# A tuned attention-and-MLP kernel in another hand-written order: which engine scales w_in, which engine forms q's long product, and the order of the loads

## The chip, the cores and the metric

The kernel runs on one core of a Trainium2 chip. The metric is the device time of one execution in microseconds, of which the median of three runs stands below. A core has five engines that work side by side, each through its own queue in order: TensorE (PE, matrix products), VectorE (DVE), ScalarE (ACT), GpSimd (POOL) and SyncE (SP, which here only issues loads and stores). An instruction that waits holds up all that stands behind it in its engine's queue.

## The reference, cut to what matters

```python
def phi(x):                                   # S1, S2: (8, 32)
    a = np.einsum('rd,bhsd->bhsr', S1, x)
    b = np.einsum('rd,bhsd->bhsr', S2, x)
    return np.einsum('bhsi,bhsj->bhsij', a, b).reshape(*x.shape[:-1], 64)
q_p, k_p = phi(q), phi(k)                     # q, k, v: (4, 4, 1088, 32)
kv  = np.einsum('bhsf,bhsd->bhfd', k_p, v)
num = np.einsum('bhsf,bhfd->bhsd', q_p, kv)
den = np.einsum('bhsf,bhf->bhs', q_p, k_p.sum(2))[..., None] + 1e-06
x   = (num / den) as 4352 tokens x 128
h   = x @ w_in                                # 128 x 2048
out = (h / (1 + exp(-beta * h))) @ w_out      # 2048 x 128
```

## The kernel before, in words

There are two parts. The **attention part** works on one batch b (0 to 3) at a time: k is loaded and transposed on VectorE (`kT`, L457), projected on TensorE (`kps`, L475), brought back on VectorE (`kab`, L489), multiplied out to 64 features on GpSimd or VectorE (`kp`, L512, in pieces of 256, 512 or 768 elements a partition), and summed against v on TensorE (`kvz`, L536). q goes the same way (`qT` L463, `qps` L596, `qab` L608, `qo` L512, `qt` L639) and ends in a product on TensorE (`nps`, L652) that is copied into the token-major input of the MLP (`xT`, L664). Batch 0 takes a shorter way for its first 512 tokens: features on TensorE (L684), a product `nps` L814, and VectorE writes `xT` (L825). In between stand the denominators: `dpr` (L616, a product of two tiles in SBUF), its sum `rc` (L626) and reciprocal (L629), and the scaling of `qab` (L634).

The **MLP part** takes nine chunks of tokens, eight of 512 and one of 256. For each chunk it goes over w_out's and w_in's 16 blocks of 128 in pairs: W (`first`, L433) is two matmuls into one of two PSUM buffers called wave, G (`silu`, L449) is ScalarE's Silu on 1024 elements a partition, V (`second`, L400) is two matmuls that add into `moeout`. There are 68 of each, and the stores of a chunk follow as E0 to E8 (L414 and L379).

Since the Silu has a factor beta, w_in is multiplied by beta ahead (`winp`, L342: eight parts of 256 columns, u + engine letter + part: `up3` is part 3 by GpSimd, `uv4` part 4 by VectorE) and w_out is divided by it (`woutp`, L351 on ScalarE as wa0 to wa15, L358 on GpSimd as wp). The first two W of a chunk read the parts 0 and 1 of `winp`, the next two 2 and 3, and so on.

What stands in which engine's queue, and in which order, is written out by hand: `SEQ` is a list of short names, the kernel calls one function for each (the table `DO`), and each call appends its instructions to its engine's queue. A name such as `v06` is batch 0's kv piece 6, `op10` the k product of batch 1, piece 0, on GpSimd, `ov10` the same on VectorE, `yp00` the q product of batch 0, piece 0, `t00` its transpose, `np0` two turns for `nps`, `nA` and `xA` the product L814 and the `xT` L825, `n0` to `n3` the products L652, `h` one matmul on a constant (L196) that only keeps TensorE busy. Loads are names too: `li0` to `li2` load w_in's columns 0 to 511, 512 to 1023 and 1024 to 2047, `lo` w_out, `lk`, `lq`, `lv` a batch of k, q, v. SyncE issues them in that order, and the program lets each load wait until the one eight places ahead of it has landed. The products `kp` have one buffer: the first of a batch waits until the `kvz` matmuls of the batch before have read the last.

Of the kernel before, what the change touches and what calls it, by code (L numbers as in the profile page):

```python
# [18 lines left out]
SEQ = """
    lqA lq0 h li0 h li1 h lk1 sp lv0 bsv h h s0 h sw h s1 tk0b be0 sk h tk0a h bc0 h li2 h h bc1 tqA  # L20
    h sr lo1 kp0 tq0 src up0 h lk2 ka0a bA up1 ka0b aA ca0a lo0 ov04 gr0 op02 cA0 ov03 ov00 h op01 h
    be1 ztv op06 gdv0 lq1 tk1 bc2 h op05 h lv1 h ca0b zm cA1 op08 h mA0 bc3 h op07 v03 v05 mA1 wm0
    kp1 zc up3 wc0 v01 rb dA ka1 up2 v02 h h iA lo2 up7 v07 v08 v00 wa6 wa7 v04 up5 qp0 lq2 wa4 wa5
    v06 gr1 qa00 kd0 op13 kda0 qa01 nd0 h gdv1 h tk2 nc0 h lv3 h nA wa2 wa3 dpp0 wm1 h op10 wc1 h xA
    wa0 wa1 np0 h di0 nca0 W op12 W tq1 G kp2 asp0 h G W ov11 h v12 uv4 lo3 G W yv00 v13 G lv2 W ka2
    yp01 h v10 t00 G v11 qp1 up6 t01 kda1 W op22 wa10 wa11 qa11 h G V qa10 op23 lk3 W np1 lq3 tq2 n0
    G dpp1 ncv1 W ov21 xa01 V xa00 op20 di1 G W V G asp1 z20 W V wp4 G W yp13 V G W z21 v23 G W yp12
    v22 G W yp10 v21 t13 zm2 G W wz2 V yp11 G t10 W v20 t12 wa12 wa13 wp7 qp2 t11 G V qa20 V kda2
    qa21 n1 E0 dpv2 V di2 xa10 V W xv11 asp2 V G tk3 W yp22 V G W tq3 kp3 G W yv21 V G W yp20 ka3 V
    G W yp23 t20 V G V W E1 np2 op32 W G t21 V ncv2 V G ov31 W V op33 t22 G W t23 V G W op30 V G W  # L30
    v33 z30 G W V G n2 z31 v31 xa21 W V G W xv20 zm3 v30 G W wz3 V G qp3 E2 v32 qa31 W V qa30 G W V
    dpv3 G W di3 V G kdv3 W asp3 V G yp31 W V G W yp32 V G W yv33 V G V yp30 W E3 np3 W G t31 V ncv3
    V G t32 W V t30 G W t33 V G W V G V W V G W V G n3 E4 W xa31 V G xv30 W V G V W V G W V G W V G
    W V G W V G W E5 V G W V G W V G V W V G W V G W V G W V G W E6 V G W V G W V G W V G W V G W V
    G W V G V W E7 V G V V V E8
"""


# [919 lines left out]
```

## Time and profile before

| | us |
|---|---|
| median of 3 runs (103.78 to 104.2) | 103.98 |
| the profiled execution | 103.7 |
| its span in the trace | 101.9 |
| busy in it: TensorE / ScalarE / VectorE / GpSimd | 96.3 / 79.1 / 64.0 / 41.0 |
| first W starts | 19.55 |
| last V ends | 98.1 |

The span is the trace from the first instruction to the last; 1.8 us of the execution's time lie around it. Before the first W lies the start (loads, beta, batch 0's k and first 512 tokens of q); behind it W, G and V alternate, and the attention of the other batches is laid between them.

### The profile page before, as it was taken

To read this page: it belongs to the slowest core of one execution; us is meant where nothing else is said; L and a number is where in the kernel's file an instruction comes from. 1 tells how busy PE (TensorE), PEld (TensorE's weight loads), DVE (VectorE), ACT (ScalarE), POOL (GpSimd) and SP (SyncE) were. 2 spreads that over 40 slices of the span, in tenths; PEclk is the share of its full clock that TensorE was granted. 3 is DMA by queue.
4 is the path that set the end of the run, shared out by engine and by line. 5 is a ranking of instruction groups with operands and counts; after the bars stand their busy time and mean duration, and the time that the engine had idled before them with its cause. 6 is when DMAs were issued, how large, how long until landed. Compare 5 with 4: busy or idle time off the path is not lost.

```text
span 101.9 us, 2974 instructions
## 1 busy us (share of the span) xinstructions
PE 96.3 (95%) x1225; PEld 48.4 (47%) x1225; DVE 64.0 (63%) x105; ACT 79.1 (78%) x110; POOL 41.0 (40%) x60
## 2 busy tenths in 40 slices
PE   5999999998999999999999999999999999999940
PEld 2465556435353454434544544454454444446730
DVE  2389989999999999995999578358032020020210
ACT  1553618699589995599997859999969999999920
POOL 7306998993976980499800001960000000000000
PEclk9999999999999999999999999999999999999996
DMA  1999999954738100330320000506012306014054
GB/s 29 306 264 385 415 398 378 358 176 149 214 71 330 68 6 0 60 52 0 57 46 6 0 9 10 90 0 103 0 19 31 60 6 100 0 24 71 8 88 67
DMA packets 23576, 11.35 MB, mean 111 GB/s; under 512 B 19323, under 2 KB 21387, under 8 KB 23563
## 3 DMA queue, kind: packets, MB, share of 16 engines
q1 hardware_dynamic: 22419, 11.08, 39.2%
q10 hardware_dynamic: 1144, 0.09, 0.8%
q8 instruction: 9, 0.15, 0.6%
q14 instruction: 4, 0.03, 0.1%
HBM read 8.94 MB, written 2.23 MB: 110 GB/s over the span
## 4 chain that ended last, share of the span: by engine, by line
PE 88%; DVE 7%; issue 0%
PE wave L433 30%; PE moeout L400 29%; PE kvz L196 8%; PE nps L652 6%; PE kvz L536 4%; PE qps L596 3%; PE kps L475 2%; DVE qo L512 1%; DVE winp L342 1%; DVE qT L463 1%; PE aps L684 1%; PE ndps L577 1%; DVE kp L512 1%; DVE kab L489 1%; PE gram L714 1%; PE kvz L714 1%
## 5 line engine op out<-in xcount | busy, mean ns | idle before, releaser
L449 ACT ACTIVATE g<-wave 128x1024 f16<-128x1024 f32 x68 | 64.8, 1036 | 4.8 <-PE wave L433 4.7
L433 PE MATMUL wave<-xT,winp 128*128 128x512 f16 (+1 forms) x144 | 40.6, 369 | 0.0
L400 PE MATMUL moeout<-g,woutp 128*128 128x512 f16 (+1 forms) x144 | 38.4, 367 | 0.1
L433 PEld LDWEIGHTS <-winp 128*128 128x128 f16 x144 | 15.2, 115 | 15.4 <-issue 5.3
L414 DVE STREAM_TRANSPOSE o_sb<-moeout 128x512 f32<-128x512 f32 (+1 forms) x9 | 6.1, 683 | 26.1 <-PE moeout L400 26.1
L400 PEld LDWEIGHTS <-woutp 128*128 128x128 f16 x144 | 13.8, 97 | 14.8 <-issue 0.8
L512 POOL TENSOR_TENSOR kp<-kab 128x256 f32<-128x256 f32 (+2 forms) x15 | 14.3, 976 | 1.9 <-DVE kab L489 1.6
L512 POOL TENSOR_TENSOR qo<-qab 128x512 f32<-128x512 f32 (+1 forms) x11 | 13.9, 1295 | 0.2
L196 PE MATMUL kvz<-idle 128*128 128x400 f16 x40 | 10.8, 381 | 1.2 <-DVE idle L115 1.1
L639 DVE STREAM_TRANSPOSE qt<-qo 128x512 f32<-128x512 f32 (+1 forms) x14 | 10.1, 753 | 0.0
L634 POOL TENSOR_TENSOR qab<-qab,rc 128x288 f32<-128x288 f32 (+1 forms) x4 | 2.5, 632 | 18.7 <-DVE rc L629 18.7
L523 DVE TENSOR_REDUCE zs<-kp 128x128 f32<-128x1152 f32 x4 | 8.4, 2145 | 0.0
L536 PEld LDWEIGHTS kvz<-kp,v 128*32 128x32 f32 x288 | 4.9, 109 | 5.7 <-issue 3.9
L536 PE MATMUL kvz<-kp,v 128*32 128x64 f32 x288 | 7.3, 224 | 0.0
L342 POOL TENSOR_TENSOR winp<-w_in_sb,beta_bc 128x256 f16<-128x256 f32 x7 | 5.1, 753 | 5.2 <-DMA w_in_sb<-in_moe_w_in_dram 5.2
L196 PEld LDWEIGHTS <-idle 128*128 128x128 f16 x40 | 3.8, 109 | 4.7 <-issue 2.5
L652 PE MATMUL nps<-qt,nd 32*32 32x288 f32 (+1 forms) x256 | 6.0, 386 | 0.0
L664 ACT CAST xT<-nps 128x576 f16<-128x576 f32 (+1 forms) x5 | 2.8, 553 | 3.7 <-PE nps L652 3.6
L463 DVE STREAM_TRANSPOSE qT<-q 128x1088 f32<-128x1088 f32 (+2 forms) x5 | 5.2, 1047 | 0.4 <-DMA q<-in_q_dram 0.4
L457 DVE STREAM_TRANSPOSE kT<-k 128x1088 f32<-128x1088 f32 (+2 forms) x5 | 5.4, 1074 | 0.0
L608 DVE STREAM_TRANSPOSE qab<-qps 128x576 f32<-128x576 f32 (+1 forms) x8 | 5.2, 683 | 0.3 <-PE qps L596 0.2
L351 ACT ACTIVATE woutp<-w_out_sb,rbeta 128x128 f16<-128x128 f32 x12 | 4.1, 396 | 1.6 <-DMA w_out_sb<-in_moe_w_out_dram 1.6
(102 smaller groups left out, 71.1 us busy)
## 6 DMA issues: line engine op xcount, KB each, us to landing
v<-in_v_dram SPq DMA_DIRECT2D x15, 144.0 KB, 5.7
k<-in_k_dram SPq DMA_DIRECT2D x3, 544.0 KB, 6.5
q<-in_q_dram SPq DMA_DIRECT2D x3, 544.0 KB, 7.5
out_dram<-o_sb SPq DMA_DIRECT2D x20, 64.0 KB, 2.0
w_out_sb<-in_moe_w_out_dram SPq DMA_DIRECT2D x4, 256.0 KB, 6.6
w_in_sb<-in_moe_w_in_dram SPq DMA_DIRECT2D x2, 256.0 KB
w_in_sb<-in_moe_w_in_dram SPq DMA_DIRECT2D x1, 512.0 KB
k<-in_k_dram SPq DMA_DIRECT2D x1, 288.0 KB, 2.8
```

The source lines that it names most:

```text
L196: nc.tensor.matmul(out=kvz0[:, HC : HC + 400], lhsT=idle, rhs=cut(idle, [[0, 25], [1, 16]]), start=fresh, stop=True, skip_group_check=True,)
L342: eng.tensor_tensor(out=winp[:, c0:c1], in0=w_in_sb[:, c0:c1], in1=beta_bc[:, c0:c1], op=MUL)
L400: nc.tensor.matmul(out=moe["acc"][:, :tw], lhsT=woutp[:, j, :], rhs=g[jj], start=(j == 0), stop=(j == NJ - 1),)
L414: nc.vector.transpose(out=o_sb[:, :nt, :].rearrange("p t d -> p (t d)"), in_=PS["acc", ci][:, :tw])
L433: nc.tensor.matmul(out=wv[:, jj // per, o : o + tw], lhsT=cut(winp, [[step, P]], c), rhs=xT[:, t0 : t0 + tw], start=True, stop=True,)
L449: nc.scalar.activation(out=g, in_=wv, func=ACTF.Silu)
L463: nc.vector.transpose(out=qT2[b % 2][:, t0:t1].rearrange("p t s -> p (t s)"), in_=q_t[b][:, t0:t1].rearrange("p t d -> p (t d)"),)
L512: eng.tensor_tensor(out=cut(dst[b][:, j0:j1], [[F, n], [R, R], [1, R]]), in0=left, in1=cut(a0, [[w, n], [0, R], [1, R]], o + R), op=MUL,)
L523: nc.vector.tensor_reduce(out=RB["zs", b][:, hs].rearrange("p h f -> p (h f)"), in_=KP[b][:, :, hs].rearrange("p j h f -> p (h f) j"), axi ...
L536: nc.tensor.matmul(out=KVZ[b][32 * h : 32 * h + 32, :F], lhsT=v_t[b][:, h, j, :], rhs=KP[b][:, j, h, :], start=(b > 0 and summed[b] == 0), ...
L639: nc.vector.transpose(out=QT[b][:, j0:j1].rearrange("p j h c s -> p (j h c s)"), in_=QO[b][:, j0:j1].rearrange("p j h f -> p (j h f)"),)
L652: nc.tensor.matmul(out=ts[g // 2][32 * h : 32 * h + 32, g % 2, : 32 * nq], lhsT=ND[b][rows, fc, 32 * h : 32 * h + 32], rhs=QT[b][rows, :nq ...
```

## The change

Only `SEQ` is changed. All functions stay, and the set of steps is nearly the same: of w_in's parts, 2, 3, 6 and 7 are now VectorE's (before: only 4), and 4 is GpSimd's; batch 0's nine k products are all GpSimd's (three were VectorE's); its long q product is GpSimd's (`yp00`); batch 0's `dpr` and scaling are VectorE's (`dpv0`, `asv0`); batch 1's `xT` is copied by ScalarE alone; three more `h`. The rest is another order. The two lists, the part up to the product `n0` of batch 0:

```diff
-    lqA lq0 h li0 h li1 h lk1 sp lv0 bsv h h s0 h sw h s1 tk0b be0 sk h tk0a h bc0 h li2 h h bc1 tqA
...
-    v06 gr1 qa00 kd0 op13 kda0 qa01 nd0 h gdv1 h tk2 nc0 h lv3 h nA wa2 wa3 dpp0 wm1 h op10 wc1 h xA
-    wa0 wa1 np0 h di0 nca0 W op12 W tq1 G kp2 asp0 h G W ov11 h v12 uv4 lo3 G W yv00 v13 G lv2 W ka2
-    yp01 h v10 t00 G v11 qp1 up6 t01 kda1 W op22 wa10 wa11 qa11 h G V qa10 op23 lk3 W np1 lq3 tq2 n0
+    lqA lq0 h li0 h lk1 h lk2 h h lv0 bsv h h tk0a be0 h tk0b sp bc0 h li2 h sk h bc1 tqA h h s1 lo0
...
+    op05 sr tk1 h src op04 h bc3 h h h bc2 lo1 op06 zm mA0 lv1 h op02 h tk2 h wm0 kp1 op07 zc wc0
+    v06 dA op03 ka1 v07 h op00 v08 iA v04 v01 v05 v03 v00 lo2 qp0 v02 gr1 lo3 qa00 kd0 qa01 nd0 h
+    lq3 gdv1 h dpv0 nc0 wa0 wa1 uv2 nA uv3 wm1 h wc1 xA h h h lq2 h di0 h h wa4 wa5 W uv7 lk3 W ca0b
+    asv0 wa2 wa3 lv2 up5 h kda0 ov10 ca0a G np0 h op13 G W h kp2 wa6 wa7 up4 W G ka2 op12 tq1 nca0 G
+    op11 v10 v12 yp00 v11 qp1 v13 W kda1 uv6 V t00 yp01 G op20 qa11 qa10 W V ov22 G V t01 wp4 W wa14
+    wa15 tq2 op23 n0 G wa10 wa11 V dpp1 xa01 np1 W op21 xa00 di1 nca1 V G V asp1 z20 W wp6 G yp12 V
```

First VectorE's queue around `xT` of the first 512 tokens (`gd` is a mask on batch 1's gram, `rc` batch 0's denominators). Before:

```order
L608 STREAM_TRANSPOSE qab<-qps 128x2x5x32 x2
L734 TENSOR_TENSOR gd_429<-gram,mh 128x32
L457 STREAM_TRANSPOSE kT_112<-k 128x1088
L825 TENSOR_TENSOR xT<-nps,rb 128x512
L626 TENSOR_REDUCE rc<-dpr_114 128x20
L629 RECIPROCAL rc<-rc 128x20
```

Of the change, the same place:

```order
L608 STREAM_TRANSPOSE qab<-qps 128x2x5x32 x2
L734 TENSOR_TENSOR gd_418<-gram,mh 128x32
L616 TENSOR_TENSOR dpr_114<-qab 128x20x8
L342 TENSOR_TENSOR winp<-w_in_sb,beta_bc 128x256 x2
L825 TENSOR_TENSOR xT<-nps,rb 128x512
L626 TENSOR_REDUCE rc<-dpr_114 128x20
L629 RECIPROCAL rc<-rc 128x20
L342 TENSOR_TENSOR winp<-w_in_sb,beta_bc 128x256
L634 TENSOR_TENSOR qab<-qab,rc 128x20x8
L512 TENSOR_TENSOR kp<-kab 128x512
L489 STREAM_TRANSPOSE kab<-kps 128x2x9x32
L463 STREAM_TRANSPOSE qT_115<-q 128x1088
```

Ahead of `xT`, batch 2's transpose of k went (it now stands earlier), and a `dpr` and two parts of `winp` (2 and 3) came; behind it come another part, the scaling and a k product.

Then GpSimd's queue from its first parts of `winp` on. Before:

```order
L342 TENSOR_TENSOR winp<-w_in_sb,beta_bc 128x256 x2
L512 TENSOR_TENSOR kp<-kab 128x256 x6
L342 TENSOR_TENSOR winp<-w_in_sb,beta_bc 128x256 x4
L512 TENSOR_TENSOR kp<-kab 128x768
L146 MEMSET v 32x64
L616 TENSOR_TENSOR dpr_114<-qab 128x20x8
L512 TENSOR_TENSOR kp<-kab 128x512 x2
L634 TENSOR_TENSOR qab<-qab,rc 128x20x8
```

Of the change:

```order
L342 TENSOR_TENSOR winp<-w_in_sb,beta_bc 128x256 x2
L512 TENSOR_TENSOR kp<-kab 128x256 x9
L342 TENSOR_TENSOR winp<-w_in_sb,beta_bc 128x256
L512 TENSOR_TENSOR kp<-kab 128x768
L342 TENSOR_TENSOR winp<-w_in_sb,beta_bc 128x256
L512 TENSOR_TENSOR kp<-kab 128x512 x2
L512 TENSOR_TENSOR qo<-qab 128x768
L512 TENSOR_TENSOR qo<-qab 128x512
```

Batch 0's products are nine instead of six, and around batch 1's 768-wide product stand two parts of `winp` and the two 512-wide products, in one row.

Last SyncE's loads, from w_in's first one (`li0`) on. Before:

```order
L167 DMA w_in_sb<-in_moe_w_in_dram 128x512 x2
L122 DMA k<-in_k_dram 128x1088
L151 DMA v<-in_v_dram 128x1x288 x4
L167 DMA w_in_sb<-in_moe_w_in_dram 128x1024
L172 DMA w_out_sb<-in_moe_w_out_dram 128x512
L122 DMA k<-in_k_dram 128x1088
```

Of the change:

```order
L167 DMA w_in_sb<-in_moe_w_in_dram 128x512
L122 DMA k<-in_k_dram 128x1088 x2
L151 DMA v<-in_v_dram 128x1x288 x4
L167 DMA w_in_sb<-in_moe_w_in_dram 128x1024
L172 DMA w_out_sb<-in_moe_w_out_dram 128x512
L167 DMA w_in_sb<-in_moe_w_in_dram 128x512
```

Batch 2's k moved up into the place of w_in's second load, which now goes out behind w_out's first and eight places behind batch 1's k.

More of the change, by code (lines that the diff above doesn't have):

```diff
@@ L19 @@
 SEQ = """
-    lqA lq0 h li0 h li1 h lk1 sp lv0 bsv h h s0 h sw h s1 tk0b be0 sk h tk0a h bc0 h li2 h h bc1 tqA
-    h sr lo1 kp0 tq0 src up0 h lk2 ka0a bA up1 ka0b aA ca0a lo0 ov04 gr0 op02 cA0 ov03 ov00 h op01 h
-    be1 ztv op06 gdv0 lq1 tk1 bc2 h op05 h lv1 h ca0b zm cA1 op08 h mA0 bc3 h op07 v03 v05 mA1 wm0
-    kp1 zc up3 wc0 v01 rb dA ka1 up2 v02 h h iA lo2 up7 v07 v08 v00 wa6 wa7 v04 up5 qp0 lq2 wa4 wa5
-    v06 gr1 qa00 kd0 op13 kda0 qa01 nd0 h gdv1 h tk2 nc0 h lv3 h nA wa2 wa3 dpp0 wm1 h op10 wc1 h xA
@@ L25 @@
-    wa0 wa1 np0 h di0 nca0 W op12 W tq1 G kp2 asp0 h G W ov11 h v12 uv4 lo3 G W yv00 v13 G lv2 W ka2
-    yp01 h v10 t00 G v11 qp1 up6 t01 kda1 W op22 wa10 wa11 qa11 h G V qa10 op23 lk3 W np1 lq3 tq2 n0
-    G dpp1 ncv1 W ov21 xa01 V xa00 op20 di1 G W V G asp1 z20 W V wp4 G W yp13 V G W z21 v23 G W yp12
-    v22 G W yp10 v21 t13 zm2 G W wz2 V yp11 G t10 W v20 t12 wa12 wa13 wp7 qp2 t11 G V qa20 V kda2
-    qa21 n1 E0 dpv2 V di2 xa10 V W xv11 asp2 V G tk3 W yp22 V G W tq3 kp3 G W yv21 V G W yp20 ka3 V
@@ L30 @@
[L30 to L34, printed above, removed]
@@ L35 @@
-    G W V G V W E7 V G V V V E8
+    lqA lq0 h li0 h lk1 h lk2 h h lv0 bsv h h tk0a be0 h tk0b sp bc0 h li2 h sk h bc1 tqA h h s1 lo0
+    s0 kp0 tq0 sw up1 aA li1 ka0b bA up0 ka0a h rb cA1 h op01 gr0 cA0 mA1 op08 h lq1 be1 gdv0 ztv
+    op05 sr tk1 h src op04 h bc3 h h h bc2 lo1 op06 zm mA0 lv1 h op02 h tk2 h wm0 kp1 op07 zc wc0
+    v06 dA op03 ka1 v07 h op00 v08 iA v04 v01 v05 v03 v00 lo2 qp0 v02 gr1 lo3 qa00 kd0 qa01 nd0 h
+    lq3 gdv1 h dpv0 nc0 wa0 wa1 uv2 nA uv3 wm1 h wc1 xA h h h lq2 h di0 h h wa4 wa5 W uv7 lk3 W ca0b
@@ new lines @@
+    asv0 wa2 wa3 lv2 up5 h kda0 ov10 ca0a G np0 h op13 G W h kp2 wa6 wa7 up4 W G ka2 op12 tq1 nca0 G
+    op11 v10 v12 yp00 v11 qp1 v13 W kda1 uv6 V t00 yp01 G op20 qa11 qa10 W V ov22 G V t01 wp4 W wa14
+    wa15 tq2 op23 n0 G wa10 wa11 V dpp1 xa01 np1 W op21 xa00 di1 nca1 V G V asp1 z20 W wp6 G yp12 V
+    W z21 V yp10 G W v23 G W yp13 E0 G zm2 v20 v21 t10 W yp11 wz2 V G t12 W V t11 G lv3 qp2 t13 v22
+    W qa21 V G qa20 V W tk3 dpp2 n1 G di2 V xa10 tq3 V asp2 xa11 W yp20 V kdv2 G W np2 yp22 G W V G
@@ new lines @@
+    yp23 W E1 kp3 G W ka3 V G t22 W op33 V ncv2 G V t23 W op30 t20 W G V op31 G W V G op32 V W yp21
+    W z30 G V G W V G t21 W v33 E2 G W z31 V G n2 zm3 xa21 W V xv20 G W wz3 V G W V G qp3 v32 qa31 W
+    V qa30 G W V dpv3 G W di3 V G W asv3 V G W E3 v31 v30 G yv32 W kdv3 yp31 V G W V yv33 G W V t32
+    G W t33 V G W yv30 V G np3 t30 W V t31 G W ncv3 V G V W E4 n3 G W xa31 V G xv30 W V G V W V G W
+    V G W V G W V G W V G W E5 V G W V G W V G W V G W V G W V G W V G W V G W E6 V G V W V G W V G
@@ L36 @@
+    W V G W V G W V G V W E7 V G V V V E8
 """
```

## The prediction, made before the changed kernel ran

> **What bounds the kernel now.** I began with the page: the share of each engine, the slices, the chain that ended last.
>
> ```profile
> PE 96.3 (95%) x1225; PEld 48.4 (47%) x1225; DVE 64.0 (63%) x105; ACT 79.1 (78%) x110; POOL 41.0 (40%) x60
> PE   5999999998999999999999999999999999999940
> DVE  2389989999999999995999578358032020020210
> ACT  1553618699589995599997859999969999999920
> POOL 7306998993976980499800001960000000000000
> PE 88%; DVE 7%; issue 0%
> ```
>
> TensorE is busy from end to end and is 88% of the chain; VectorE's 7% must lie somewhere, and the chain in order of time says where. Its columns are start, duration and what ran; I took one row from each turn.
>
> ```profile
> 18.75 0.69 DVE xT L825
> 23.12 1.41 DVE qo L512
> 26.61 0.18 PE kvz L196
> 28.20 1.10 PE nps L652 x58
> 65.04 0.48 PE wave L433 x2
> 65.52 0.43 PE moeout L400 x2
> 74.03 1.53 PE nps L652 x63
> 98.13 0.45 DVE o_sb L414
> ```
>
> The chain passes through VectorE at `xT`, which lets the first W go, and in the stretch behind it. From 28.20 on it is TensorE alone. So I cut the span at three marks (first W, end of batch 0's product, end of batch 3's) and asked for the busy time of each stretch: length, then TensorE, its weight loads, VectorE, ScalarE, GpSimd.
>
> ```profile
> 19.55:29.31 9.76, 9.22 (x208) 4.39 (x207) 9.73 (x13) 8.21 (x12) 7.85 (x9) 1.00 0.55 172
> 29.31:75.56 46.25, 46.23 (x593) 21.66 (x594) 36.16 (x50) 39.99 (x46) 19.81 (x19) 1.00 0.23 49
> 75.56:98.13 22.57, 22.53 (x117) 11.89 (x116) 2.91 (x5) 21.20 (x23) 0.00 (x0) 1.00 0.25 39
> ```
>
> Behind 29.31 TensorE has no gap worth the name, and the granted clock (third from last) is 1.00. The matmuls behind the first W are the same in both programs. So the kernel's end is the start of the first W, plus a nearly fixed 78.58 us, and the change is decided by what happens to `xT` near 18.75. What can be won behind it is 0.54 us of gaps in the first stretch, and what W pairs of 0.48 lose against 0.43 (0.05 each, a dozen between 61 and 74: 0.6).
>
> **The change part by part: the start.** Now the instructions just ahead of the first W, from the timeline, on all engines.
>
> ```profile
> 16.09 0.32 PE L536 MATMUL kvz<-kp,v 128*32 128x64 f32 x8
> 16.34 0.77 PE L714 MATMUL gram<-kab 128*64 128x32 f32 x18
> 16.58 1.51 POOL L512 TENSOR_TENSOR kp<-kab 128x768 f32<-128x768 f32 x1 [0.28 <-POOL winp L342]
> 17.15 0.19 DVE L734 TENSOR_TENSOR gd<-gram,mh 128x32 f32<-128x32 f32 x1
> 17.98 0.66 PE L814 MATMUL nps<-qp,nd 64*32 64x256 f32 x16
> 18.75 0.69 DVE L825 TENSOR_TENSOR xT<-nps,rb 128x512 f16<-128x512 f32 x1 [0.19 <-PE nps L814]
> 19.55 1.03 PE L433 MATMUL wave<-xT,winp 128*128 128x512 f16 x4
> 20.18 4.92 ACT L449 ACTIVATE g<-wave 128x1024 f16<-128x1024 f32 x5 [0.23 <-PE wave L433]
> 10.01 3.54 POOL L512 TENSOR_TENSOR kp<-kab 128x256 f32<-128x256 f32 x6
> ```
>
> Before, batch 0's kvz ends at 16.41, GpSimd's 768-wide product starts 0.17 later because it takes the buffer that those matmuls read, gram ends near 17.11, VectorE's `gd` follows at 17.15, and `xT` waits for `nps` only.
>
> In the change GpSimd makes nine products in place of six: 10.01 + 9 x 3.54 / 6 = 15.32, and the last kvz must follow them. TensorE's own list (the same matmuls, be1 and qps at other places) comes there at 16.2 to 16.5. I take 16.5: no term. The three more `h` (0.18 each at 26.61 above) lie in the same list ahead of the first W, two of them in its wait for `xT`; without that wait they would cost 0.2 to 0.5. The `nps` then ends near 18.5, 0.2 earlier than before.
>
> What is new is VectorE's queue: `dpr` and two `winp`, all with both inputs in SBUF, stand ahead of `xT`, while GpSimd runs products. The trace of before has that meeting once, at 21 to 24.5.
>
> ```profile
> 20.90 0.47 POOL L634 TENSOR_TENSOR qab<-qab,rc 128x160 f32<-128x160 f32 x1
> 21.09 0.82 DVE L512 TENSOR_TENSOR kp<-kab 128x512 f32<-128x512 f32 x1
> 21.44 1.39 POOL L512 TENSOR_TENSOR qo<-qab 128x512 f32<-128x512 f32 x1
> 21.84 1.28 DVE L342 TENSOR_TENSOR winp<-w_in_sb,beta_bc 128x256 f16<-128x256 f32 x1
> 22.80 0.92 POOL L342 TENSOR_TENSOR winp<-w_in_sb,beta_bc 128x256 f16<-128x256 f32 x1
> 23.04 1.49 DVE L512 TENSOR_TENSOR qo<-qab 128x768 f32<-128x768 f32 x1
> ```
>
> Read the ends: GpSimd's 21.37, VectorE's 21.91, GpSimd's 22.83, VectorE's 23.12, GpSimd's 23.72, VectorE's 24.53. The two never work together; each starts, stands until the other's instruction ends, and then takes 0.54 (512 wide), 0.92 (512 on GpSimd), 0.29 (`winp` on VectorE), 0.60 (`winp` on GpSimd), 0.81 (768). They take strict turns. The `winp` that took 1.28 worked for 0.29 of it.
>
> Put into the change: GpSimd's 768-wide product starts at 16.5 + 0.17 = 16.67 and ends at 18.18. VectorE reaches `dpr` behind `gd`, near 17.4, and stands until 18.18. 160 elements at the rate of 0.54 for 512 and 0.29 for 256 are some 0.19: 18.37. GpSimd's next `winp` has been standing: 18.97. VectorE's first `winp`: 19.26. GpSimd's 512-wide product: 20.18. The second `winp`: 20.47. Only then `xT`, 0.69, and the first W 0.11 behind it (19.55 after 19.44): 21.27 in place of 19.55. The term is **+1.7 us**. Its lower end is -0.2, if no turn is waited for and `xT` starts with `nps`; its upper end +2.6, if w_in's late load makes VectorE lose a turn (below). I take the value nearest to the six rows above.
>
> SBUF — State Buffer, section "Who interferes with whom", in the Trainium skill, says that a VectorE instruction with two SBUF inputs contends with a GpSimd instruction that reads SBUF, and that whoever issues first holds the shared interface for the whole instruction; the six ends above agree. By it the sum is 1.7 us later; by GPSIMD Engine Reference, section "Elementwise — side-by-side cycle accounting", which has VectorE about twice as fast as GpSimd at this work (4497 ns against 2293 ns), moving `winp` to VectorE shortens the start, and the sum would be the first rival's.
>
> **Behind the first W.** To the end of `n0` the change runs seven W and three V, before seven W and one V: two V, 0.86 at 0.43 each, are done sooner. But VectorE's order now puts batch 2's `kab` ahead of q's transpose, so that it stands until `kps` of batch 2, which waits on TensorE for the third W, and that for the first G, which gives a wave buffer back (a G starts 0.63 behind the first W, as 20.18 after 19.55, and takes 4.92 / 5 = 0.98: free near 22.9). By the rows' durations `kps` ends near 24.3, `kab` (0.77) at 25.1, q's transpose (1.25) at 26.3, and `n0` near 31.6 to 31.7. Against 29.31 + 0.86 that is 1.4 to 1.5 late: **-0.2** out of the 0.54 gap. From there to the end nothing is left out of TensorE's list; batch 1's second `xT` copy goes to ScalarE (0.64 a piece) behind the first one, covered by two V (0.86); without that cover 0.4 is lost. Against it stand the 0.6 of W pairs. I put both at **0**. ScalarE has six `woutp` (4.1 / 12 = 0.34 each) and three copies of some 0.3 to 0.4 ahead of the first G, some 3.1 from 17.8 on: done near 21, some 0.9 before the first G can start (19.55 to 20.18 is 0.63, so 21.9). With `xT` on time they would hold it for a microsecond.
>
> ```profile
> L351 ACT ACTIVATE woutp<-w_out_sb,rbeta 128x128 f16<-128x128 f32 x12 | 4.1, 396 | 1.6 <-DMA w_out_sb<-in_moe_w_out_dram 1.6
> L664 ACT CAST xT<-nps 128x576 f16<-128x576 f32 x3 | 1.9, 638 | 3.3 <-PE nps L652 3.3
> L463 DVE STREAM_TRANSPOSE qT<-q 128x1088 f32<-128x1088 f32 x3 | 3.8, 1261 | 0.0
> L489 DVE STREAM_TRANSPOSE kab<-kps 128x576 f32<-128x576 f32 x3 | 2.3, 775 | 0.3 <-PE kps L475 0.3
> ```
>
> **The loads.** w_in's second part is needed by VectorE at 18.97. It goes out when batch 1's k has landed, eight places ahead.
>
> ```profile
> 10.69 0.33 SPq L172 DMA_DIRECT2D w_out_sb<-in_moe_w_out_dram  x1
> SPq L172 <- DMA k<-in_k_dram: 1.1, 1, 1.1
> w_out_sb<-in_moe_w_out_dram SPq DMA_DIRECT2D x4, 256.0 KB, 6.6
> q<-in_q_dram SPq DMA_DIRECT2D x3, 544.0 KB, 7.5
> ```
>
> Before, the load behind that k went out at 10.69, and 256 KB took 6.6 us: 17.3, or 18.2 with the 7.5 that a load of q took at the most. That is 0.8 to 1.7 us of cover. Batch 2's k is read by VectorE near 12.8, one batch's load after the k that landed by 10.69: covered, and 0 if late by less than the 3 us till its product.
>
> **The sum.** +1.7 - 0.2 = +1.5 on the profiled 103.7: 105.2. The median of the runs shown lies 0.28 above that execution (103.98); with half of that I say 105.3.
>
> **The rivals.**
> 1. *No turns are waited for.* If GpSimd's 768-wide product came before VectorE's `dpr` and its next ones later, or a `winp` could run beside a product, `dpr` and two `winp` take 0.19 + 2 x 0.29 = 0.77, from 17.45 to 18.2, hidden beside `nps`. Then the first W starts at 19.35, 0.2 earlier, and 0.2 more comes from the gaps: **103.3**, provided that ScalarE is through its list by 20; if it holds the first G till 21, the time is near 104, with rival 2. The rival decides from the point where the two instructions cost under 1.1 us together with `dpr` (18.53 less 17.45). For it: a single `winp` works for 0.29. Against it: the 768-wide product waits for kvz and `dpr` for gram, right behind kvz on TensorE, so they meet by construction. By the rule of the GPSIMD Engine Reference above it would be the likeliest.
> 2. *The delay is given back.* V stand ready earlier, so W pairs at 0.48 shrink to 0.43 (0.6) and the 0.54 of gaps is filled wholly: 1.7 - 1.1 leaves 0.6, at the edge of what counts: **104.0 to 104.3**. Against it: 46.23 busy of 46.25.
> 3. *w_in comes late.* If it lands behind 18.97, GpSimd takes its 512-wide product first and the second one ahead of the second `winp`: 0.92 later: **106.2**.
>
> **Chances.** Forecast (104.6 to 106.0) 0.69, rival 1 0.13, rival 2 0.11, rival 3 0.07. The range leaves out most of rival 1 and nothing else of weight: 103.5 to 106.3. A measurement of this kernel tells about 0.5% from no change (103.46 to 104.5): faster 0.14, same 0.12, slower 0.74.
>
> **What would show it.** In the changed profile `winp` on VectorE should take well over 0.29 twice, ending on GpSimd's ends; `xT` L825 should start near 20.4, the first G near 21.9, and batch 0's `nps` L652 end near 31.6. A first W before 20 makes the prediction wrong by its main term; a first W at 21.2 and an end under 99 by the second.

## The result, and the profile after

The changed kernel is slower: 107.25 us (median of 4 runs, 106.99 to 107.31) against 104.09 of the kernel before beside it. The ratio is 1.0309, with a 95% interval of 1.0275 to 1.0343. I had forecast 105.3 and a range of 103.5 to 106.3: the direction was right, the size was not, and the time lies above the range. One of the four runs beside it was a slow one (106.33); such runs count in the medians given here and below, and not in the ratios. The profiled execution took 107.31, its span is 105.5 (before: 103.7 and 101.9).

First the page of the changed kernel: the shares, TensorE's slices, and the chain by engine.

```profile
PE 97.5 (92%) x1228; PEld 49.4 (47%) x1228; DVE 62.8 (59%) x105; ACT 79.1 (75%) x111; POOL 40.8 (39%) x59
PE   5999999867999799999999999999999999999950
PE 62%; POOL 6%; ACT 2%; issue 0%; DVE 0%; POOLq 0%
```

A slice is 2.64 us here. TensorE's row of nines is broken in the 8th to 10th slice (18.5 to 26.4 us) and once more in the 14th (34.3 to 36.9); before, a single 8 stood in it. The shares add up to 70% only, because the chain is followed back to 27.2 and no further. New in it is GpSimd with 6%, which was absent before.

Then the same three stretches as in the prediction, cut at the first W, the end of batch 0's product and the end of batch 3's.

```profile
21.90:32.32 10.42, 9.42 (x210) 4.73 (x209) 8.56 (x14) 8.15 (x13) 6.77 (x7) 1.00 0.40 142
32.32:79.17 46.85, 45.89 (x595) 21.68 (x592) 34.10 (x48) 40.95 (x48) 19.40 (x20) 1.00 0.20 37
79.17:101.80 22.63, 22.53 (x117) 11.88 (x116) 2.98 (x5) 21.20 (x23) 0.00 (x0) 1.00 0.24 39
```

Beside those of before, the first W is 2.35 later (21.90 against 19.55), the first stretch 0.66 longer (10.42 against 9.76) and the second 0.60 (46.85 against 46.25): together 3.61, which is the whole delay of the last V (it starts at 99.93 against 96.32). The third is no longer than before: its mark 101.80 was set 0.07 too late, for the copy of the last result, at whose start the stretch before was cut (98.13), starts at 101.73. The second stretch shows something that the sum had no place for. TensorE is busy 0.34 less than before, as fewer V are left, and still needs 0.60 more: 0.96 of it is idle, where before it was 0.02.

The start, instruction by instruction (start, duration, engine, what ran, and in brackets the idle time ahead of it and what ended it):

```profile
17.00 0.32 PE L536 MATMUL kvz<-kp,v 128*32 128x64 f32 x8
17.48 1.51 POOL L512 TENSOR_TENSOR kp<-kab 128x768 f32<-128x768 f32 x1 [1.38 <-PE kvz L536]
18.16 1.01 DVE L616 TENSOR_TENSOR dpr<-qab 128x160 f32<-128x160 f32 x1
18.63 0.67 PE L814 MATMUL nps<-qp,nd 64*32 64x256 f32 x16
18.95 0.81 POOL L342 TENSOR_TENSOR winp<-w_in_sb,beta_bc 128x256 f16<-128x256 f32 x1
19.10 2.15 DVE L342 TENSOR_TENSOR winp<-w_in_sb,beta_bc 128x256 f16<-128x256 f32 x2
19.72 2.45 POOL L512 TENSOR_TENSOR kp<-kab 128x512 f32<-128x512 f32 x2
21.17 0.68 DVE L825 TENSOR_TENSOR xT<-nps,rb 128x512 f16<-128x512 f32 x1
21.90 1.02 PE L433 MATMUL wave<-xT,winp 128*128 128x512 f16 x4 [1.13 <-DVE xT L825]
22.33 0.36 DVE L342 TENSOR_TENSOR winp<-w_in_sb,beta_bc 128x256 f16<-128x256 f32 x1
```

The turns are there, and one can read them from the ends: GpSimd's product ends at 18.99, VectorE's `dpr` 0.18 behind it, GpSimd's `winp` 0.59 behind that, and the two `winp` on VectorE take 2.15 where a single one on its own takes 0.36 (the last row). `nps`, for which `xT` had waited before, is done at 19.3: VectorE is 1.9 late for it. But everything stands 0.6 to 0.8 later than I had put it, from kvz on, which ends at 17.3 and not at 16.5.

### The profile page after: what moved, and what is told of

It reads as the page before. It is cut to its first block, busy times and chain, and to the rows that moved or that the text cites. A ratio compares the mean times of both kernels' runs of the same rounds, so it can differ in the third digit from the quotient of the medians.

```text
span 105.5 us, 2973 instructions
## 1 busy us (share of the span) xinstructions
PE 97.5 (92%) x1228; PEld 49.4 (47%) x1228; DVE 62.8 (59%) x105; ACT 79.1 (75%) x111; POOL 40.8 (39%) x59
## 4 chain that ended last, share of the span: by engine, by line
PE 62%; POOL 6%; ACT 2%; issue 0%; DVE 0%; POOLq 0%
PE wave L433 26%; PE moeout L400 25%; PE nps L652 4%; POOL kp L512 3%; PE kvz L536 3%; PE qps L596 2%; ACT g L449 2%; POOL woutp L358 2%; POOL dpr L616 1%; POOL qab L634 1%; PE kps L475 1%; PE kvz L548 1%; DVE o_sb L414 0%; PE ndps L577 0%; POOLq L512 0%
## 5 line engine op out<-in xcount | busy, mean ns | idle before, releaser
L512 POOL TENSOR_TENSOR kp<-kab 128x256 f32<-128x256 f32 (+2 forms) x19 | 17.5, 949 | 5.5 <-PE kvz L536 4.2
L512 POOL TENSOR_TENSOR qo<-qab 128x512 f32<-128x512 f32 (+1 forms) x11 | 13.2, 1222 | 13.0 <-DVE qab L634 13.0
L196 PE MATMUL kvz<-idle 128*128 128x400 f16 x43 | 11.6, 397 | 1.1 <-DVE idle L115 1.1
L639 DVE STREAM_TRANSPOSE qt<-qo 128x512 f32<-128x512 f32 (+1 forms) x14 | 10.3, 761 | 0.0
L536 PE MATMUL kvz<-kp,v 128*32 128x64 f32 x288 | 6.6, 222 | 0.7 <-ACT nd L586 0.7
L196 PEld LDWEIGHTS <-idle 128*128 128x128 f16 x43 | 4.4, 114 | 4.8 <-issue 2.4
L652 PE MATMUL nps<-qt,nd 32*32 32x288 f32 (+1 forms) x256 | 6.0, 386 | 0.0
L342 POOL TENSOR_TENSOR winp<-w_in_sb,beta_bc 128x256 f16<-128x256 f32 x4 | 3.0, 749 | 5.2 <-DMA w_in_sb<-in_moe_w_in_dram 5.2
L664 ACT CAST xT<-nps 128x576 f16<-128x576 f32 (+1 forms) x6 | 3.4, 567 | 1.9 <-PE nps L652 1.9
L489 DVE STREAM_TRANSPOSE kab<-kps 128x576 f32<-128x576 f32 (+2 forms) x5 | 3.2, 654 | 2.6 <-PE kps L475 2.6
L652 PEld LDWEIGHTS nps<-qt,nd 32*32 32x32 f32 x256 | 3.2, 103 | 2.5 <-issue 1.2
```

Of the source, the lines that this page charges most:

```text
L196: nc.tensor.matmul(out=kvz0[:, HC : HC + 400], lhsT=idle, rhs=cut(idle, [[0, 25], [1, 16]]), start=fresh, stop=True, skip_group_check=True,)
L512: eng.tensor_tensor(out=cut(dst[b][:, j0:j1], [[F, n], [R, R], [1, R]]), in0=left, in1=cut(a0, [[w, n], [0, R], [1, R]], o + R), op=MUL,)
L536: nc.tensor.matmul(out=KVZ[b][32 * h : 32 * h + 32, :F], lhsT=v_t[b][:, h, j, :], rhs=KP[b][:, j, h, :], start=(b > 0 and summed[b] == 0), ...
L639: nc.vector.transpose(out=QT[b][:, j0:j1].rearrange("p j h c s -> p (j h c s)"), in_=QO[b][:, j0:j1].rearrange("p j h f -> p (j h f)"),)
L652: nc.tensor.matmul(out=ts[g // 2][32 * h : 32 * h + 32, g % 2, : 32 * nq], lhsT=ND[b][rows, fc, 32 * h : 32 * h + 32], rhs=QT[b][rows, :nq ...
```

## The experiments

The theory after the result had three parts, one for each stretch: the turns ahead of `xT` and late kvz (2.35), an order behind the first W that holds batch 2's `kps` and q's transpose (0.66), and V that were done early for nothing (0.60). Each has its rivals, and 13 runs bear on them. Where a sentence says "the end", it is the start of the last row of 16 V matmuls in the chain: 96.32 before, 99.93 in the changed kernel. The start of `n0` is that of its product L652: 28.13 before, 31.21 in the changed kernel. First the two rows before, then those of the change:

```profile
28.13 1.17 PE L652 MATMUL nps<-qt,nd 32*32 32x160 f32 x64
96.32 1.78 PE moeout L400 x16
```

```profile
31.21 1.17 PE L652 MATMUL nps<-qt,nd 32*32 32x160 f32 x64
99.93 1.78 PE moeout L400 x16
```

### The start: turns, and idle matmuls

**`dpr` and the two `winp` behind `xT`** (names as in `SEQ`; a line for the place before and one for after):

```diff
-gdv1 h dpv0 nc0 wa0 wa1 uv2 nA uv3 wm1 h wc1 xA h h h
+gdv1 h nc0 wa0 wa1 nA wm1 h wc1 xA uv2 uv3 dpv0 h h h
```

> The changed kernel with VectorE's dpr and two winp moved from ahead of xT (L825) to right behind it; nothing left out. Theory 1 (the first W is late because VectorE stands for GpSimd's turns ahead of xT): xT starts when nps L814 ends, near 19.3, the first W near 20.0 in place of 21.9; if the first W sets the end, 1.9 less: 105.3. Rival 1a (what bounds behind it is VectorE's whole queue up to q's transpose, which is as long as before): first W at 20.0 too, but the third W waits for winp, batch 0's nps L652 ends at most 0.9 earlier, time 106.3 to 107.0. Rival 1b (the start decides, not the queue): first W within 0.4 of 21.9 and the time within 0.4 of 107.25.

Measured: 106.43, ratio 1.0193 (1.0136 to 1.025). From its timeline, on TensorE, VectorE and ScalarE (its line numbers stand one higher):

```profile
18.99 0.69 DVE L826 TENSOR_TENSOR xT<-nps,rb 128x512 f16<-128x512 f32 x1 [1.15 <-PE nps L815]
19.60 2.18 DVE L343 TENSOR_TENSOR winp<-w_in_sb,beta_bc 128x256 f16<-128x256 f32 x2
20.20 1.03 PE L434 MATMUL wave<-xT,winp 128*128 128x512 f16 x4
21.11 1.92 ACT L450 ACTIVATE g<-wave 128x1024 f16<-128x1024 f32 x2
30.16 1.17 PE L653 MATMUL nps<-qt,nd 32*32 32x160 f32 x64 [0.17 <-DVE qt L640]
```

`xT` waits for `nps` again and the first W is 1.70 earlier. Of this, 0.41 is the execution's: its kvz, with the same list ahead of it, ends at 16.91 in place of 17.32. The move itself is worth 1.29. That the row of `dpr` and two `winp` delays `xT` is shown. But n0 starts only 1.05 earlier (30.16 against 31.21) and the end 1.42 (98.51). The first G starts 0.91 behind the first W in place of 0.63, since ScalarE's list of `woutp` and copies lasts till 21.1, and the two `winp` still take 2.18, now in the row that leads to q's transpose.

**The same move made in the kernel before**: `dpr` and the parts 2 and 3 taken from GpSimd and put ahead of `xT` on VectorE.

```diff
-zc up3 wc0
+zc wc0
-ka1 up2 v02
+ka1 v02
-h lv3 h nA wa2 wa3 dpp0 wm1 h op10 wc1 h xA
+h lv3 h dpv0 uv2 nA wa2 wa3 uv3 wm1 h op10 wc1 h xA
```

> The kernel before with one piece of the change alone: dpr and winp parts 2 and 3 are VectorE's and stand ahead of xT (they were GpSimd's); nothing left out. Theory 1: VectorE stands for GpSimd's 768- and 512-wide products, xT starts near 20.7 in place of 18.75, first W near 21.5, time 1.5 to 2.5 more than before: 105.6 to 106.6. Rival 1b (turns are not what made xT late): the three instructions take 0.2 to 0.4 each, xT starts by 19.6, time within 0.5 of before.

Measured: 105.87, ratio 1.013 (1.0065 to 1.0195). Its profiled execution ran at a lowered TensorE clock (0.978), so I read only VectorE's rows from it.

```profile
19.70 1.62 DVE L342 TENSOR_TENSOR winp<-w_in_sb,beta_bc 128x256 f16<-128x256 f32 x2
21.24 0.68 DVE L825 TENSOR_TENSOR xT<-nps,rb 128x512 f16<-128x512 f32 x1
```

`xT` starts at 21.24 in place of 18.75. Two `winp`, 0.36 each on their own in the changed kernel, take 1.62 in turns, behind a `dpr` that ends at 19.77, and this move alone makes the kernel before 1.3% slower.

**13 of the idle matmuls out** ahead of the first W, in the changed kernel (they feed nothing, so nothing is left uncomputed):

```diff
-bc0 h li2 h sk h bc1 tqA h h s1
+bc0 h li2 sk h bc1 tqA s1
-ka0a h rb cA1 h op01
+ka0a rb cA1 op01
-op08 h lq1
+op08 lq1
-tk1 h src op04 h bc3 h h h bc2
+tk1 src op04 h bc3 bc2
-lv1 h op02 h tk2 h wm0
+lv1 op02 h tk2 wm0
-v07 h op00
+v07 op00
```

> The changed kernel with 13 of the h (L196, matmuls on a constant) between sps and batch 0's last kvz taken out; they compute nothing that is used. Theory 2 (TensorE's list ahead of batch 0's last kvz is full, and its order with more h ahead makes kvz end at 17.3 in place of 16.4): kvz ends when GpSimd's ninth product allows it, near 16.2, GpSimd's 768-wide product and VectorE's turns move with it, first W near 21.0, time 0.8 to 0.9 less: 106.4. Rival 2 (the h fill waits only, or keep TensorE's clock up): kvz ends within 0.2 of 17.3, time unchanged or longer, granted clock lower between 6 and 17.

Measured: 106.76, ratio 1.0244 (1.018 to 1.0309). From the timeline:

```profile
16.13 0.32 PE L536 MATMUL kvz<-kp,v 128*32 128x64 f32 x8
16.61 1.51 POOL L512 TENSOR_TENSOR kp<-kab 128x768 f32<-128x768 f32 x1 [0.60 <-issue]
21.02 1.02 PE L433 MATMUL wave<-xT,winp 128*128 128x512 f16 x4 [1.13 <-DVE xT L825]
```

kvz ends at 16.45, GpSimd's 768-wide product starts at 16.61 (I had 16.67), the first W at 21.02 (I had 21.27), and the end comes 0.88 earlier. In the changed kernel kvz ends 2.42 behind GpSimd's ninth product, which is done at 14.90; here it ends 1.12 behind it (15.33), and TensorE waits for GpSimd's products (0.24 and 0.26). So in the profiled execution the late kvz lay on TensorE's own list, which has 25 `h` ahead of it, against 23 before.

It is not always so. With the list of the change ahead of it, kvz ends at 16.91 to 17.51 in seven programs, and in three of them 1.12 or 1.13 behind GpSimd's ninth product: there GpSimd's row is last, which begins when w_in's first load lands (its first `winp` starts at 8.22 to 9.72 in the seven). And the interval of this run's ratio overlaps that of the changed kernel, so that the gain in time is likely and not shown.

**Both together**, `xT` first and the 13 idle matmuls out: the edits of the first and the third experiment.

> The changed kernel with both mends at once: dpr and two winp behind xT, and 13 h out; nothing that is used is left out. If turns ahead of xT (1.4 carried to the end in the trace of a_x_first) and the fuller list of TensorE (0.9) are separate causes, they add: span 103.2 in place of 105.5, ratio to before 1.008 to 1.013. Rival: they overlap (GpSimd's products then run at another time against VectorE's), ratio 1.016 or more.

Measured: 105.84, ratio 1.0188 (1.0138 to 1.0238), no better than the first alone and not the 1.008 to 1.013 of causes that add. A table by stretches shows a part of why (length, TensorE, weight loads, VectorE, ScalarE, GpSimd, then the granted clock):

```profile
8.00:10.00 2.00, 1.90 (x60) 1.33 (x53) 1.45 (x5) 0.77 (x2) 1.11 (x2) 1.00 1.02 411
10.00:15.00 5.00, 4.85 (x82) 2.72 (x86) 4.94 (x8) 1.95 (x7) 5.00 (x10) 0.76 1.06 397
```

Here the granted clock fell to 0.76 in the profiled execution, and the first W starts at 20.21, as with the idle matmuls in. With the same 13 out, the third experiment kept 1.00 in that stretch, in which TensorE was busy less:

```profile
10.00:15.00 5.00, 4.47 (x110) 2.86 (x108) 4.92 (x8) 2.19 (x8) 5.00 (x10) 1.00 1.05 395
```

The clock is not all of it. In the run with all repairs, further down, the same 13 are out, the clock is 1.00 in that stretch, and the first W still starts at 20.27: GpSimd's nine products end at 15.85 there, and kvz 1.13 behind them.

Idle matmuls cost time here, and leaving them out goes with a lower clock: the mean granted clock was under 0.985 in 7 of the 34 executions of the five programs with 9 or 13 of them out, and in 1 of 102 of the others. What tips it in the one execution and not in the other stays open.

### From the first W to n0: two chains, then VectorE

**Batch 2's `kps` right behind the second W, and batch 0's `nd` earlier on ScalarE:**

```diff
-W uv7 lk3 W ca0b
+W uv7 lk3 W kp2 ca0b
-op13 G W h kp2 wa6 wa7 up4 W G ka2 op12 tq1 nca0 G
+op13 G nca0 W h wa6 wa7 up4 W G ka2 op12 tq1 G
```

> The changed kernel with two links of the stretch behind the first W mended together: batch 0's copy nd ahead of two woutp (frees the buffer of batch 1's kvz), and batch 2's kps right behind the second W, so that VectorE reaches q's transpose sooner; nothing left out. Theory 4 (two chains side by side, each hiding the other, so that the one alone in a_nca_wp6 won nothing): qps of batch 1 starts near 26.1 in place of 27.3, batch 0's nps L652 ends 1.0 to 1.3 earlier, time 0.8 to 1.3 less, ratio 1.018 to 1.024. Rival 4 (the next wait, woutp by GpSimd, zs, or ScalarE, takes it all): nps earlier, ratio 1.028 to 1.034.

Measured: 106.22, ratio 1.0218 (1.0183 to 1.0253). On TensorE:

```profile
22.09 1.02 PE L433 MATMUL wave<-xT,winp 128*128 128x512 f16 x4 [1.13 <-DVE xT L825]
23.04 0.72 PE L475 MATMUL kps<-kT,sk 64*32 64x288 f32 x16
30.30 1.18 PE L652 MATMUL nps<-qt,nd 32*32 32x160 f32 x64
```

From the first W to n0 it takes 8.21 in place of 9.31. In the changed kernel `kps` comes 2.40 behind the first W (24.30), here 0.95. The first W itself was 0.19 later in this execution.

**`nd` earlier alone, and a `woutp` of GpSimd's earlier**, without moving `kps`:

```diff
-op13 G W h kp2
+op13 G nca0 W h kp2
-op12 tq1 nca0 G
+op12 tq1 G
-dpp1 xa01 np1 W op21 xa00
+dpp1 wp6 op21 xa01 np1 W xa00
-z20 W wp6 G
+z20 W G
```

> The changed kernel with two steps moved: ScalarE's copy nd of batch 0 (which frees the PSUM buffer of batch 1's kvz) ahead of two woutp, and GpSimd's woutp of the blocks 12 and 13 ahead of a 512-wide k product; nothing left out. Theory 3 (the two gaps of TensorE at 25.5 and 34.9, 0.7 and 0.6, are lost for good): 0.6 to 1.3 less, 106.0 to 106.6. Rival 3 (what is won is waited for later, at q's transpose and where the W wait for ScalarE): both gaps gone but the time within 0.3 of 107.25.

Measured: 107.9, ratio 1.034 (1.0282 to 1.0398): nothing gained. The edits aim at two waits on TensorE in the changed kernel, 0.57 for `woutp`, shown further down, and 0.71 for `nd`:

```profile
26.27 0.88 PE L536 MATMUL kvz<-kp,v 128*32 128x64 f32 x48 [0.71 <-ACT nd L586]
```

Both are gone, and two others stand in their place (line numbers one higher again):

```profile
26.93 0.78 PE L597 MATMUL qps<-qT,sw 32*32 32x288 f32 x32 [0.94 <-DVE qT L464]
38.60 0.25 PE L549 MATMUL kvz<-zs,ones 128*32 128x64 f32 x2 [1.03 <-DVE zs L524]
```

So TensorE's wait for `nd` was not the whole cause: two chains end side by side there, TensorE's through `nd` and VectorE's through `kps`, `kab` and q's transpose. `nd` moved without `kps` gains nothing, both moved together gain 1.10 between the first W and n0. `kps` alone was not run, so that it takes both is not shown.

**All repairs at once**: `xT` first, 13 idle matmuls out, `kps` and `nd` earlier, and two copies on ScalarE that nothing reads left out.

```diff
-ca0b asv0 wa2 wa3
+asv0 wa2 wa3
-kda0 ov10 ca0a G
+kda0 ov10 G
```

> The changed kernel with all mends: xT first, 13 h out, nd earlier, kps of batch 2 earlier, and ScalarE's two copies a0, which nothing reads, out. If the three causes add: 2.2 and another 0.8 to 1.3 less, ratio 0.996 to 1.004. Rival (something further in the new order costs): ratio over 1.01, and a wait behind 32 us that before does not have.

Measured: 105.88, ratio 1.0179 (1.0147 to 1.0212), with n0 at 30.10 and the end at 98.46. That is no better than `xT` first alone (1.0193) and far from the 0.996 to 1.004 of causes that add. TensorE's row names what is left:

```profile
21.22 0.72 PE L475 MATMUL kps<-kT,sk 64*32 64x288 f32 x16
25.82 0.78 PE L596 MATMUL qps<-qT,sw 32*32 32x288 f32 x32 [0.92 <-DVE qT L463]
30.10 1.17 PE L652 MATMUL nps<-qt,nd 32*32 32x160 f32 x64
```

`kps` is done at 21.9 and `qps` still comes at 25.82, behind a wait for q's transpose: VectorE's own row, with two `winp` of 2.18 in turns in it, is the bound.

**The two `winp` given back to GpSimd**, with `xT` first, `kps` and `nd` earlier, and the idle matmuls in. (`nd` is ScalarE's, not VectorE's as the expectation has it.)

```diff
-gdv1 h dpv0 nc0 wa0 wa1 uv2 nA uv3 wm1 h wc1 xA h h h
+gdv1 h nc0 wa0 wa1 nA wm1 h wc1 xA dpv0 h h h
-W uv7 lk3 W ca0b
+W lk3 W kp2 ca0b
-op13 G W h kp2 wa6 wa7 up4 W G ka2 op12 tq1 nca0 G
+op13 up2 up3 G nca0 W h wa6 wa7 W G ka2 op12 tq1 G
-v13 W kda1 uv6 V t00 yp01 G
+v13 up4 W kda1 V t00 yp01 uv7 uv6 G
```

> The changed kernel with dpr and the three winp of the change behind xT, two of the three given back to GpSimd (behind batch 1's k products), and with batch 2's kps right behind the second W and batch 0's nd earlier on VectorE; the idle matmuls stay in. Theory 6: once the first W is early, VectorE's own row from xT to q's transpose is the next bound, and the two winp in it, 2.18 in turns in the run with xT first, are its largest part that can go. Then n0 starts at 28.5 to 29.5 and the ratio is 1.003 to 1.012. Rival: something else than VectorE holds n0 (TensorE's W and kps, or GpSimd, which now has two more winp ahead of its products); then n0 starts near 30.1 as in the run with all three repairs (30.10) and the ratio is 1.016 to 1.020.

Measured: 105.03, ratio 1.0082 (1.005 to 1.0114). On TensorE, with the chain's last V:

```profile
29.29 1.18 PE L652 MATMUL nps<-qt,nd 32*32 32x160 f32 x64
97.65 1.78 PE moeout L400 x16
```

n0 at 29.29 and the ratio lie where theory 6 had them. Against the run with all repairs n0 is 0.81 earlier (30.10 to 29.29), with the idle matmuls in. The edit gives two parts of w_in to the other engine; it also moves the parts 4, 6 and 7 back, 7 out of the same row of VectorE's. The run does not part the two, but in that row the two had taken 2.18 and part 7 0.36. With this run, 2.3 of the 3.1% have been taken out again by moving eight names.

### Behind n0: V done early

**The two V put back**, from ahead of n0 to the places near 53 and 56 where TensorE waits for g:

```diff
-qa11 qa10 W V ov22 G V t01 wp4 W
+qa11 qa10 W ov22 G t01 wp4 W
-yp13 E0 G zm2 v20 v21 t10 W yp11 wz2 V G t12 W V t11 G
+yp13 G zm2 v20 v21 t10 W yp11 wz2 V G t12 W V E0 t11 G
-yp23 W E1 kp3 G W ka3 V G t22 W op33 V ncv2 G
+yp23 W kp3 G W ka3 V G t22 W op33 V E1 ncv2 G
-op30 t20 W G V op31
+op30 t20 W G V V op31
-W z30 G V G W
+W z30 G V V G W
```

> The changed kernel with the two V that it has more ahead of n0 taken out there and put back at 53 and 56 us, where TensorE waits for ScalarE's g (chunks 0 and 1 are put out two V later for it). Theory 5: the two V done early are worth nothing, since TensorE stands about 0.57 for woutp and 0.4 for g behind n0; n0 starts at 31.2 as in the changed kernel, both waits go, and the end comes within 0.3 of the changed kernel's (span 105.2 to 105.8, ratio 1.027 to 1.034). Rival: TensorE's work not yet done at n0 sets the end, as I credited it; then the two V cost 0.86 again behind n0 (span 106.1 to 106.5, ratio 1.036 to 1.042).

Measured: 108.79, ratio 1.0445 (1.0393 to 1.0496). Neither theory had this, and the run is no clean test: the outputs E0 and E1 had to move with their V, and they made waits of their own, on VectorE ahead of batch 1's products (0.43) and on the single accumulator (0.81).

```profile
37.99 0.25 PE L548 MATMUL kvz<-zs,ones 128*32 128x64 f32 x2 [0.44 <-DVE zs L523]
53.11 0.59 PE L400 MATMUL moeout<-g,woutp 128*128 128x512 f16 x2 [0.81 <-DVE o_sb L414]
```

One reading stands: with two V less to do up to there, TensorE comes through the matmuls on `zs` no sooner, since it waits 0.44 for `zs`. The last two of them start 16.58 behind the first W here and in the changed kernel.

**Two V done early in the kernel before**, where TensorE has no gap behind n0 and no output has to move:

```diff
-qa11 h G V qa10 op23 lk3 W np1
+qa11 h G V qa10 V op23 lk3 V W np1
-W ov21 xa01 V xa00 op20 di1 G W V G asp1
+W ov21 xa01 xa00 op20 di1 G W G asp1
```

> The kernel before with two V (V2 and V3) moved from behind n0 to ahead of it, as the change has them. TensorE has no gap there (n0 starts at 28.13 without a wait) and none behind. Credit as I took it: n0 starts 0.7 to 0.9 later, the stretch behind it is 0.86 shorter, the end stays within 0.15 (ratio 0.999 to 1.002; from n0 to the last x16 67.3 to 67.5). Rigid stretch: n0's start sets the end whatever V are done (68.2 in eight runs so far), and the end moves with n0: ratio 1.006 to 1.009, n0 to the last x16 68.0 to 68.3, with new waits of TensorE behind n0 that add up to 0.6 or more.

Measured: 104.72, ratio 1.0061 (1.0031 to 1.0092). On TensorE, with the chain's last V:

```profile
28.77 1.18 PE L652 MATMUL nps<-qt,nd 32*32 32x160 f32 x64
30.92 0.59 PE L433 MATMUL wave<-xT,winp 128*128 128x512 f16 x2 [0.41 <-ACT xT L664]
31.84 0.59 PE L433 MATMUL wave<-xT,winp 128*128 128x512 f16 x2 [0.33 <-ACT g L449]
96.82 1.78 PE moeout L400 x16
```

n0 starts 0.64 later than before, and from there to the end it takes 68.05 against 68.19. Of the 0.86 of V, 0.73 is paid ahead of n0 (9.31 from the first W to it, 8.58 before), and the gain behind it is eaten by waits of 0.74. What holds TensorE there is ScalarE: the wait of 0.41 is for its copy of n0's own product (`xT`), that of 0.33 for a G. Its row of G behind that copy is already closed in the kernel before (eight G in 7.68, from 30.12 on), and here it is the same row, 0.64 later (eight in 7.54, from 30.76 on):

```profile
30.12 7.68 ACT L449 ACTIVATE g<-wave 128x1024 f16<-128x1024 f32 x8
```

The next W needs a wave buffer, which only a G gives back. V that are out of the way do not bring the next W sooner. The credit was wrong. (The expectation's 68.2 was 68.18 to 68.72 in ten of the programs so far, and 69.31 and 70.69 in two.)

**GpSimd's two `woutp` ahead of batch 1's k products**, in the changed kernel:

```diff
-yp01 G op20
+yp01 wp4 wp6 G op20
-t01 wp4 W wa14
+t01 W wa14
-z20 W wp6 G
+z20 W G
```

> The changed kernel with GpSimd's two woutp products moved up: from between batch 1's k products to ahead of them, where GpSimd stands 2.8 for kvz. Theory 7: behind n0 the chain from batch 0's last kvz through GpSimd's products (28.73 to 34.07) to zs on VectorE and to batch 1's kvz sets when TensorE gets its work, and the V done early only brought TensorE sooner to its waits. With one woutp less in it that chain is some 0.9 shorter, and TensorE's wait of 0.57 for woutp is gone: from batch 0's n0 to the last x16 some 68.2 in place of 68.72 (ratio 0.005 under the changed kernel's, near 1.026). Rival: ScalarE's g between 47 and 61 holds TensorE in any case; then the 0.57 comes back there as longer waits for g, and the stretch stays at 68.6 to 68.8 (ratio 1.030 to 1.033).

Measured: 106.83, ratio 1.0235 (1.0199 to 1.0271). For comparison the two `woutp` in the chain of the changed kernel, in which GpSimd's row runs without a gap worth the name from 28.73 to 35.38, and TensorE's row behind it:

```profile
29.80 1.02 POOL woutp L358
34.80 0.58 POOL woutp L358
```

```profile
35.43 0.60 PE L400 MATMUL moeout<-g,woutp 128*128 128x512 f16 x2 [0.57 <-POOL woutp L358]
```

And GpSimd, TensorE and the chain's last V in the experiment:

```profile
25.67 1.18 POOL L358 TENSOR_TENSOR woutp<-w_out_sb,rbeta 128x256 f16<-128x256 f32 x2
31.01 1.18 PE L652 MATMUL nps<-qt,nd 32*32 32x160 f32 x64
99.17 1.78 PE moeout L400 x16
```

The two products now run while GpSimd stands anyway, the wait of 0.57 is gone, and from n0 to the end it takes 68.16 in place of 68.72. Theory 7 had 68.2. Of the 0.60 that the second stretch lost, this is nearly all.

### Versions that beat both kernels

**Nine idle matmuls out of the kernel before:**

```diff
-src up0 h lk2
+src up0 lk2
-ov03 ov00 h op01 h be1
+ov03 ov00 op01 be1
-bc2 h op05 h lv1 h ca0b
+bc2 op05 lv1 h ca0b
-op08 h mA0 bc3 h op07
+op08 mA0 bc3 op07
-v02 h h iA
+v02 iA
```

> The kernel before with 9 h out between batch 0's kab and its last kvz; they compute nothing that is used. If TensorE's list bounds that part there too (window 12.3 to 16.4 without a gap): kvz ends 0.5 to 0.9 earlier, ratio 0.991 to 0.996. Rival (VectorE's row kab, kp, zt, kT, qp is as full, or the clock falls): ratio 0.998 to 1.003.

Measured: 103.7 against 104.08, ratio 0.9943 (0.9914 to 0.9972). n0 starts at 27.48, the end is 95.66. The first W is only 0.21 earlier (19.34); the other 0.44 lies between it and n0, where VectorE's one `winp` takes 0.68 in place of 1.28. Whether that is the reason was not tried by itself.

**And its one `winp` on VectorE given to GpSimd**, `uv4` to `up4` at the same place (`ov11 h v12 uv4 lo3`), the change's step reversed:

> The kernel before with nine idle matmuls out, as in the run that beat both kernels, and with its one winp on VectorE (between batch 1's k product and q's product, 0.68 to 1.28 in turns) given to GpSimd at the same place: the change's step in the other direction. Theory 6 (VectorE's row from xT to q's transposes bounds n0, and turns lie in it): n0 starts 0.3 to 0.7 earlier than the 27.48 of that run, ratio 0.988 to 0.992. Rival: GpSimd's qo, which the winp now pushes back by 0.5 to 0.9, becomes the late one (VectorE's qt needs it), or the fourth W waits for the winp: n0 27.3 to 27.9, ratio 0.993 to 0.998.

Measured: 103.28 against 104.23, ratio 0.9893 (0.9864 to 0.9922). In its profiled execution the start was late (mean clock 0.991), so the length counts and not the place:

```profile
19.91 1.03 PE L433 MATMUL wave<-xT,winp 128*128 128x512 f16 x4
27.81 1.17 PE L652 MATMUL nps<-qt,nd 32*32 32x160 f32 x64
```

From the first W to n0 it takes 7.90, against 8.14 with the idle matmuls alone out and 8.58 before; from n0 to the end (95.99) 68.18. The ratio came out where theory 6 had it; the place of n0 did not, for 27.81 lies in the rival's range (27.3 to 27.9). This is the fastest version of the study. Its interval and that of the one before touch (0.9914 to 0.9922), so that the `winp` adds to the gain is likely and not shown.

## Why the prediction was wrong, step by step

- **What bounds the kernel: right in kind.** The end followed the first W and the row behind it in every run. But the "nearly fixed 78.58 us" behind the first W were not fixed: they are 79.83 in the changed kernel. What I had not seen is which point sets the end. From the start of n0 to the end it takes 68.05 to 68.72 in 12 of the 14 programs compared (the lowered clock's aside), the kernel before (68.19) and the changed one (68.72) among them. The two others are the run with moved outputs and the one with the wait for `zs`.
- **Turns ahead of `xT`, +1.7: right in mechanism, too small.** It measures +2.35. The turns took what I had worked out (from the 768-wide product's start to `xT`'s 3.69, predicted 3.80). The failed figure is "the last kvz ... I take 16.5: no term": it ended at 17.32, and at 16.91 to 17.51 in the seven programs with that list. I had priced the `h` at 0.2 to 0.5 if the wait for `xT` gave no cover, and left that out, though the cover is not there for kvz, on which GpSimd's turn hangs. Nor are they three: ahead of the first W the change has 34 against 30, two of the four ahead of kvz. Without 13 of them kvz ended at 16.45. In other executions it is GpSimd's nine products, which hang on w_in's first load, that come last ahead of kvz.
- **Behind the first W, -0.2: wrong, and this is the larger error.** The first half of the step was right: n0's end 10.3 behind the first W was predicted, 10.42 is measured, by the chain that I had named: `qps` waits 0.16 for q's transpose. (The chain through `nd`, which ends beside it, I had not seen.) Against it I set "two V, 0.86 at 0.43 each, are done sooner". The runs show no worth in them: put in ahead of n0 in the kernel before, they come back as 0.74 of waits for ScalarE. In the changed kernel itself no run shows it so cleanly. So the term is +0.66, and not -0.2.
- **Behind n0, 0: wrong by 0.60.** 0.57 of it is GpSimd's `woutp`, laid into batch 1's row of products; moving it gives 0.56 back. I had costed the steps "from there to the end" by TensorE's list alone and had not followed GpSimd's queue behind the moved names. The 0.6 of W pairs that I set against it was a misreading too: between 61 and 74 the chain has six of them, not a dozen, at 0.47 to 0.49, 0.29 in all above 0.43.
- **The three errors add up.** The first W 0.63 behind its forecast (21.90 against 21.27), the credit of 0.86 and 0.60 behind n0 make 2.09; 3.61 measured less 1.52 predicted (1.72 and -0.2) is 2.09.
- **The rivals.** No turns: wrong, `winp` took 2.15 for two. Given back later: wrong, and the reverse is true, for the early V are lost. w_in late: VectorE did not wait for its second load; GpSimd waited 0.48 for the third at 15.38, ahead of a wait for kvz of 1.38 that hides it. The range reached 106.3 by this rival alone: what was missing was a case in which the credit is worth nothing.

The two rules of the Trainium skill that the prediction weighed came out apart. SBUF — State Buffer, section "Who interferes with whom", has the two engines exclude each other for whole instructions, and the changed trace agrees (2.15 for two `winp`, 0.36 for one on its own). GPSIMD Engine Reference, section "Elementwise — side-by-side cycle accounting", has VectorE about twice as fast at such work; that holds for the one `winp` on its own (0.36, against 0.72 for GpSimd's at 15.38) and says nothing of the two in turns.
